# Zeroing a row table in smaller pieces, moving four scatters behind the last x, and turning step 2's rows ahead of w1's load

## The chip, the cores and the metric

The kernel runs on one core of a Trainium2 chip. The metric is the device time of one execution in microseconds (us). A kernel is compared by the median of several runs; one further execution is profiled, and the trace is of that one. The engines are PE (matrix products and transpositions), DVE (vector), ACT (activations and copies), POOL (GpSimd; it also issues the indirect DMAs) and SP (it issues the plain DMAs and the DMA transpositions, in order, waiting where it must).

## What is computed

Linear attention with exponential random features (batch 8, 8 heads, 576 tokens, head size 64, 128 features), and on its output a mixture of 8 experts where each of the 4608 tokens goes to one expert.

```python
phi = lambda x: exp(h - max(h)) / sqrt(m)        # h = x @ omega.T - |x|^2/2
kv  = einsum('bhsm,bhsd->bhmd', phi(k), v);  z = phi(k).sum(axis=2)
out = (phi(q) @ kv) / (phi(q) @ z + 1e-6)        # -> x: (4608, 512)
logits = x @ w_gate;  e = argmax(logits, axis=1);  g = softmax(logits)[e]
y[mask_e] = g[mask_e] * (relu(x[mask_e] @ w1[e]) @ w2[e])      # for each expert e
```

## The kernel before

**Attention.** `Attention.run` goes through 8 batches of 4 head pairs. Each engine's instructions run in the order in which the code is written. Of a batch, 512 tokens of each head are worked on per head (`unit_*`), the last 64 tokens of all heads together (loads `kr`, `qr` in `load_rest`, L127). k, q and v come in 256 KB loads (`load_part`, L131; `load_v`, L149) that SP issues a batch ahead into two sets of buffers. PE turns k and q (`turns`, L158), ACT copies them out (L200) and takes the exponentials (L241), POOL sums the key features (L257), DVE makes x (`pair_x`, L324 to 326), POOL copies x into rows `xr` and `xc` (L333, L336).

**Routing.** For each batch DVE and PE work out each token's expert and its place in that expert's part of a table in DRAM, `rows_by_expert` (8 parts of 4992 rows, 2056 bytes each). POOL scatters the rows of a batch into it, 128 rows to an indirect DMA (`place`, L664); `rt.move()` issues the next such scatter, so four or five belong to a batch. Not every row of a part gets a token, and the tables' rows that are read directly are zeroed before: `Experts.clear(1)`, in the batch with number 1, lets POOL zero a buffer `xg[1]` (L835) and one third of `xg[0]` (L836), and SP write `xg[1]` eight times into the table (L838).

**Experts.** `Experts.run` works in steps of up to 256 rows. Step 0 has the first 256 rows of the largest expert, step 1 the next 256 (`second`, L842, a plain DMA that waits for the scatters). From step 2 on POOL gathers a step's rows by a list of indices (`gather`, L958, two tiles of 128 rows; `gather3` a third tile) into `xg[t % 2]`. SP turns each tile by a DMA transposition (`flips`, L868) into `xt`; ACT joins the halves (`xtrans`, L976) and rounds them (`xh`, L58), DVE takes the rest (`xl`, L52). `marks(t)` copies a step's gate values (POOL, L986) and token numbers (DVE, L987) and needs all its tiles. PE makes layer 1 (L1005) and layer 2 (L1046 to 1048), with DVE splitting `w2` (L52) and making `hl` (L1020) during step 1. `next` loads the next expert's weights, 2 MB each (`dma1`, L928: w1; `dma2`, L931: w2). Results leave by scatters (L1080).

In step t, `step` issues the turning of step t + 1; `begin(t + 1)` reads it after layer 1 of step t.

Of the kernel before, what the change touches and what calls it, by code (L numbers as in the profile page):

```python
# [9 lines left out]
F32 = mybir.dt.float32  # L10
# [10 lines left out]
P = 128  # L21
B, H, S, D, M = 8, 8, 576, 64, 128
DM = H * D
E, F = 8, 1024
NT = B * S
SM = 512
SR = S - SM
NJ = SM // P
NP = H // 2
# [8 lines left out]
RW = 2 * DM + 4  # L38
# [25 lines left out]
class Attention:  # L64
# [340 lines left out]
    def pair(self, i, p, pre):  # L405

        rt, (u, w) = self.routing, self.units[i:i + 2]
        self.unit_p(*u)
        self.unit_m(*u)
        self.warm(5 * (p == 2))  # L410
        self.turns(i + 3, i - 2, pre)
        self.copies(i + 3, i - 2, pre)
        for k in range(2):
            pre.ahead(i + k - len(self.units))
        products = bool(rt.queue) and rt.queue[0] in rt.pe
        rt.some(int(products))
        rt.some(1, False)
        self.pair_kv(p - 1)
        self.pair_kvt(p - 1, self.nc.vector.tensor_copy)
        rt.some(2 + (p > B * NP - 3) - products, False)  # L420
        self.unit_e(*u, 0)
        self.pair_fold(p - 2)
        self.unit_e(*u, 1)
        self.unit_ks(*u)
        rt.move()
        self.unit_p(*w)
        self.unit_m(*w)
        self.turns(i + 4, i - 1, pre)
        self.copies(i + 4, i - 1, pre)
        self.unit_e(*w, 0)  # L430
        self.unit_e(*w, 1)
        rt.exps()
        self.unit_ks(*w)
        rt.move()
        if p % NP < NP - 1 or p == B * NP - 1: self.numbers(p - 2)

    def run(self, pre):
        self.units = [(b, h) for b in range(B) for h in [-1] + list(range(H))]
        n, rt = len(self.units), self.routing
        self.start()  # L440
        for b in range(B):
            i = b * (2 * NP + 1)
            if b:
                self.rest(i, b, pre)
                pre.clear(b)
            if b + 1 < B:
                self.load_rest(b + 1)
                self.load_main(b + 1)
            for k in range(0 if b else 2, NP):
                self.pair(i + 1 + 2 * k, b * NP + k, pre)  # L450
                if k == (0 if b else 2) and b + 1 < B:
                    self.load_v(b + 1)
        p = B * NP - 1
        self.cq.close()
        bank = lambda name: self.pt.tile([P, 2, 2, NJ * D], F32, name=name, tag="tt")
        tt = bank("tt_end")
        self.pair_kv(p)
        self.pair_kvt(p)
        self.ci.close()
        pre.banks()  # L460
        assert not rt.queue
        self.turn_q(n - 2, tt[:, :, 1])
        self.qt(n - 2, tt[:, :, 1])
        self.pair_fold(p - 1)
        self.pair_fold(p, "kv")
        rt.move(2)
        self.pair_nu(p - 1, 0)
        self.pair_x(p - 1, 0)
        self.turn_q(n - 1, tt[:, :, 0])
        self.qt(n - 1, tt[:, :, 0], self.nc.scalar.copy)  # L470
        self.pair_nu(p - 1, 1)
        self.pair_x(p - 1, 1)
        last = bank("nu_end")
        pre.fill(2)
        for a in range(2):
            self.pair_nu(p, a, last[:, a].rearrange("p k c -> p (k c)"))
        for a in range(2):
            self.pair_x(p, a)
        assert len(rt.moves) == 0
        self.ct.close()  # L480
        pre.banks2()


class Routing:
# [69 lines left out]
    def bank(self, name):  # L554
        return self.ps.tile([P, 512], F32, name=name, tag=self.tag)
# [252 lines left out]
class Experts:  # L808
# [22 lines left out]
        self.idx = [cp.tile([P, 3], U32, name=f"idx{i}") for i in range(3)]  # L831

    def clear(self, k):
        if k == 1:
            self.nc.gpsimd.memset(self.xg[1].rearrange("p a c -> p (a c)").bitcast(F32), 0.0)  # L835
            self.nc.gpsimd.memset(self.xg[0][:, 2].bitcast(F32), 0.0)  # L836
            for x in self.table.rearrange("(e n) c -> e n c", e=E):
                self.nc.sync.dma_start(x[self.T2:self.T2 + self.T3].rearrange("(a p) c -> p a c", p=P), self.xg[1])  # L838

    def second(self):  # L840
        rows = self.table.rearrange("(e n) c -> e n c", e=E)[bass.ds(self.first, 1), self.T2:2 * self.T2]
# [100 lines left out]
    def split(self, n, cs=range(8)):  # L942
        for c in cs:
            split_r(self.nc, *self.part(n, c), self.nc.scalar, self.nc.vector)
# [163 lines left out]
    def step(self, t, following, split=lambda: None):  # L1108
        engines = (ET.PE, ET.DVE, ET.Activation, ET.Pool)
        if t + 1 < NPR:  # L1110
            self.flips(t + 1)
            self.flips3(t + 1)
        split()
        kind = self.kind(t, engines)
        self.l1(t, kind)
        if t + 2 < NPR:
            self.gather(t + 2)
            self.gather3(t + 2)
        if t == 1:
            self.next(0, 2)  # L1120
        following()
        self.nc.gpsimd.drain()
        with self.tc.If(kind > 1) as pair:
            self.l2(t, 0)
            self.when(self.reg(4, t, 1, engines), lambda: self.l2(t, 1))
        with pair.Else():
            with self.tc.If(kind > 0) as short:
                self.l2half(t)
            with short.Else():
                self.l2(t, 2)  # L1130
            for a in range(2):
                self.l2(t, a)
# [11 lines left out]
    def run(self, ctx):  # L1144
        nc, rt = self.nc, self.rt
# [26 lines left out]
        self.l20(0)  # L1172
        self.xtrans(1)
        self.low(range(4, 8), nc.vector)
        self.next(0, 1)
        self.gather(2)
        self.gather3(1)
        self.marks(1)
        self.l20(1)
        self.flips3(1)  # L1180
        self.third(1)
# [49 lines left out]
```

## Time and profile before

| | |
|---|---|
| runs of the kernel before | 691.11, 692.62, 693.4 us; median 692.62 |
| the profiled execution | 690.93 us, of which the span of the trace is 689.2 us |
| mean granted clock of PE | 0.982 of full speed |
| busy share of the span | PE 94%, ACT 57%, DVE 48%, POOL 44% |
| attention | 0 to about 257 us |
| last routing, scatters, step 0 | about 257 to 285.6 us |
| steps from 1 on | 285.6 us to the end |

Times in the rows are us from the start of the span. In attention PE and ACT are both busy nearly all the time; in the steps PE alone is.

### The profile page before, as it was taken

What the parts mean: (1) busy time and instruction counts of PE and PEld (TensorE: products, weight loads), DVE (VectorE), ACT (ScalarE), POOL (GpSimd) and SP (SyncE); (2) the same over time, 40 slices, a digit from 0 to 9 for tenths busy, and PEclk for the clock granted to TensorE, in tenths of its full rate; (3) what the DMA queues carried; (4) which work ended last, traced back from release to release, by engine and by line L of the source; (5) the groups of instructions that cost most, each with busy time, mean ns of one, the idle gap of its engine ahead of it and who ended that gap; (6) DMA issues with size and microseconds to landing.
All of it is one profiled execution on the core that took longest, in us unless ns stands there. A gap on an engine that the chain in (4) does not pass through costs nothing. (4 is left out here: it accounts for less than half of the span.)

```text
span 689.2 us, 19218 instructions
## 1 busy us (share of the span) xinstructions
PE 646.5 (94%) x7123; PEld 584.5 (85%) x7123; DVE 330.7 (48%) x782; ACT 395.6 (57%) x971; POOL 300.6 (44%) x495
## 2 busy tenths in 40 slices
PE   8994999999999979986999989999999999999996
PEld 7993989898898967676889888899899899889894
DVE  3472777878877858632222235421236237222220
ACT  6993999999999953522342345431454446342421
POOL 6572698888888884321222121323201321332121
PEclk9997999999999999998999999999999999999998
DMA  8749957557474263697554025855207926843001
GB/s 219 200 170 307 258 148 235 166 161 206 134 218 157 116 196 113 172 181 188 124 101 95 31 65 169 214 118 116 62 23 192 240 64 179 245 113 51 31 18 39
DMA packets 111101, 100.55 MB, mean 146 GB/s; under 512 B 67358, under 2 KB 91934, under 8 KB 110944
## 3 DMA queue, kind: packets, MB, share of 16 engines
q1 hardware_dynamic: 100656, 68.66, 39.5%
q0 software_dynamic: 9744, 29.71, 13.8%
q8 instruction: 92, 1.51, 0.9%
q14 instruction: 65, 0.53, 0.3%
q10 hardware_dynamic: 544, 0.13, 0.1%
HBM read 64.35 MB, written 26.41 MB: 132 GB/s over the span
## 5 line engine op out<-in xcount | busy, mean ns | idle before, releaser
L1005 PE MATMUL p<-xh,w1p 128*128 128x256 f32 (+2 forms) x960 | 148.3, 297 | 5.9 <-ACTq L1085 5.2
L1005 PEld LDWEIGHTS p<-xh,w1p 128*128 128x128 f32 x960 | 135.5, 189 | 8.7 <-ACTq L1085 5.6
L1019 ACT ACTIVATE hh<-p 128x512 fp32r<-128x512 f32 (+2 forms) x84 | 43.8, 522 | 132.6 <-PE p L1005 120.8
L1080 POOL DMA_INDIRECT out_dram<-ys,idx x32 | 33.7, 1055 | 181.5 <-DVE ys L1076 90.7
L1020 DVE SCALAR_TENSOR_TENSOR hl<-p,hh 128x512 fp32r<-128x512 f32 (+2 forms) x84 | 48.1, 576 | 120.0 <-ACT hh L1019 112.4
L229 DVE TENSOR_REDUCE mx<-pp 128x8 f32<-128x1024 f32 x64 | 78.2, 1221 | 29.7 <-PE pp L222 26.6
L241 ACT ACTIVATE qp<-pp,mx 128x128 f32<-128x128 f32 x256 | 85.2, 564 | 0.0
L241 ACT ACTIVATE kp<-pp,mx 128x128 f32<-128x128 f32 x256 | 83.3, 528 | 2.2 <-DVE de L324 0.9
L1005 PE MATMUL p<-xl,w1p 128*128 128x256 f32 (+2 forms) x480 | 83.3, 295 | 0.0
L200 ACT COPY tq<-tt 128x1024 f32<-128x1024 f32 x59 | 69.9, 1184 | 15.0 <-PE tt L158 14.9
L222 PE MATMUL pp<-om_t,tq 64*128 64x128 f32 x1024 | 75.0, 286 | 1.5 <-ACT tq L203 0.7
L1005 PEld LDWEIGHTS p<-xl,w1p 128*128 128x128 f32 x480 | 70.5, 189 | 0.0
L222 PEld LDWEIGHTS pp<-om_t,tq 64*128 64x128 f32 x1024 | 62.8, 188 | 5.3 <-ACT qp L241 2.0
L958 POOL DMA_INDIRECT xg<-rows_by_expert,src x49 | 52.7, 1075 | 24.6 <-issue 23.3
L257 POOL TENSOR_TENSOR k<-kp 128x256 f32<-128x256 f32 x64 | 46.6, 728 | 35.1 <-ACT kp L241 34.1
L976 ACT COPY xw<-xt 128x1024 uint16<-128x1024 uint16 x36 | 48.6, 1349 | 15.3 <-DMA xt<-xg 15.3
L52 DVE TENSOR_TENSOR xl<-xw,xh 128x512 fp32r<-128x512 f32 x36 | 24.9, 693 | 57.7 <-ACT xh L58 49.2
L1080 POOL DMA_INDIRECT out_dram<-y,idx x6 | 6.0, 1004 | 105.7 <-DVE y L1076 57.0
L1048 PE MATMUL p_t<-w2p,hl 128*128 128x512 f32 x120 | 47.0, 392 | 1.4 <-issue 1.4
L1046 PE MATMUL p_snu<-w2p,hh 128*128 128x512 f32 x120 | 47.0, 392 | 0.4 <-issue 0.4
L1048 PE MATMUL p_snu<-w2p,hl 128*128 128x512 f32 x120 | 47.0, 391 | 0.0
L1046 PE MATMUL p_t<-w2p,hh 128*128 128x512 f32 x120 | 46.8, 390 | 0.0
(372 smaller groups left out, 1274.3 us busy)
## 6 DMA issues: line engine op xcount, KB each, us to landing
w1s<-in_moe_w_dram SPq DMA_DIRECT2D x5, 2048.0 KB
w2s<-in_moe_w_dram SPq DMA_DIRECT2D x5, 2048.0 KB
v<-in_v_dram SPq DMA_DIRECT2D x32, 256.0 KB
k<-in_k_dram SPq DMA_DIRECT2D x31, 256.0 KB
q<-in_q_dram SPq DMA_DIRECT2D x31, 256.0 KB
rows_by_expert<-xg SPq DMA_DIRECT2D x8, 771.0 KB
xg<-rows_by_expert SPq DMA_DIRECT2D x2, 514.0 KB
kr<-in_k_dram SPq DMA_DIRECT2D x16, 64.0 KB
```

The costliest lines, as they stand in the source:

```text
L200: self.nc.scalar.copy(self.pack(i, j), tt)
L222: nc.tensor.matmul(pp[:, a, n, i, :], th[r, k].rearrange("p a t -> p (a t)"), self.om[r, :], start=True, stop=True)
L229: nc.vector.tensor_reduce(out=mx[:, :, n], in_=s[("pp", h)][:, :, n], axis=AX.X, op=ALU.max, negate=True)
L241: nc.scalar.activation(x[:, j, :], pp[:, j % 2, n, j // 2, :], AF.Exp, bias=mx[:, j % 2, n, j // 2:j // 2 + 1])
L257: add = lambda o, x, y: nc.gpsimd.tensor_tensor(out=o, in0=x, in1=y, op=ALU.add)
L958: self.nc.gpsimd.indirect_dma_start(out=self.xg[t % 2][:, a], out_offset=None, in_=self.table, in_offset=bass.IndirectOffsetOnAxis(ap=self ...
L976: self.nc.scalar.copy(x.bitcast(U16).rearrange("p c (t k) -> p k c t", k=2), xt.rearrange("p (k c) t -> p k c t", k=2))
L1005: self.nc.tensor.matmul(o, w[:, i, c], x[:, i, :], start=k == 0, stop=k == len(ops) - 1)
L1019: self.nc.scalar.activation(a[:, :, :n], o[:, :, :n], AF.Relu)
L1020: low = lambda d, c: self.nc.vector.scalar_tensor_tensor(out=d, in0=o[:, :, c], scalar=0.0, in1=a[:, :, c].bitcast(F32), op0=ALU.max, op1= ...
L1046: nc.tensor.matmul(p, h, self.w2h[:, c, :], start=c == 0, stop=False)
L1048: nc.tensor.matmul(p, l, self.w2h[:, c, :], start=False, stop=c == self.NF - 1)
```

## The change

There are three parts.

1. The zeroed rows of each expert's part are 288 to 511 (224 rows, one DMA of 112 partitions by 2 rows) where they were 256 to 639 (384 rows). They are written by `blank(p)` ahead of the pairs 2 to 7, that is in the batches with numbers 0 and 1: one, one, one, two, two and one DMA. Their source is one tile of `xg[1]`, which POOL zeroes at the start; the rest of the buffers is zeroed in the batches 2 and 3.
2. In the last pair `move` issues nothing; the four scatters of the seventh batch (number 6) follow after POOL's last copies of x, ahead of the last batch's.
3. `flips(2)` stands ahead of w1's load, `next(0, 1)`, and no longer in `step(1)`.

```diff
--- before.py
+++ after.py
@@ -422,7 +422,7 @@
         self.pair_fold(p - 2)
         self.unit_e(*u, 1)
         self.unit_ks(*u)
-        rt.move()
+        rt.move(int(p < B * NP - 1))
         self.unit_p(*w)
         self.unit_m(*w)
         self.turns(i + 4, i - 1, pre)
@@ -431,7 +431,7 @@
         self.unit_e(*w, 1)
         rt.exps()
         self.unit_ks(*w)
-        rt.move()
+        rt.move(int(p < B * NP - 1))
         if p % NP < NP - 1 or p == B * NP - 1: self.numbers(p - 2)
 
     def run(self, pre):
@@ -442,11 +442,12 @@
             i = b * (2 * NP + 1)
             if b:
                 self.rest(i, b, pre)
-                pre.clear(b)
+            pre.clear(b)
             if b + 1 < B:
                 self.load_rest(b + 1)
                 self.load_main(b + 1)
             for k in range(0 if b else 2, NP):
+                pre.blank(b * NP + k)
                 self.pair(i + 1 + 2 * k, b * NP + k, pre)
                 if k == (0 if b else 2) and b + 1 < B:
                     self.load_v(b + 1)
@@ -463,7 +464,6 @@
         self.qt(n - 2, tt[:, :, 1])
         self.pair_fold(p - 1)
         self.pair_fold(p, "kv")
-        rt.move(2)
         self.pair_nu(p - 1, 0)
         self.pair_x(p - 1, 0)
         self.turn_q(n - 1, tt[:, :, 0])
@@ -476,7 +476,8 @@
             self.pair_nu(p, a, last[:, a].rearrange("p k c -> p (k c)"))
         for a in range(2):
             self.pair_x(p, a)
-        assert len(rt.moves) == 0
+        rt.move(NJ)
+        assert not rt.moves
         self.ct.close()
         pre.banks2()
 
@@ -831,11 +832,21 @@
         self.idx = [cp.tile([P, 3], U32, name=f"idx{i}") for i in range(3)]
 
     def clear(self, k):
-        if k == 1:
-            self.nc.gpsimd.memset(self.xg[1].rearrange("p a c -> p (a c)").bitcast(F32), 0.0)
-            self.nc.gpsimd.memset(self.xg[0][:, 2].bitcast(F32), 0.0)
-            for x in self.table.rearrange("(e n) c -> e n c", e=E):
-                self.nc.sync.dma_start(x[self.T2:self.T2 + self.T3].rearrange("(a p) c -> p a c", p=P), self.xg[1])
+        zero = self.nc.gpsimd.memset
+        if k == 0:
+            zero(self.xg[1][:, :1].bitcast(F32), 0.0)
+        elif k == 2:
+            zero(self.xg[1][:, 1:].bitcast(F32), 0.0)
+        elif k == 3:
+            zero(self.xg[0][:, 2].bitcast(F32), 0.0)
+
+    def blank(self, p):
+
+        known = NT // 2 // E
+        n = (2 * self.T2 - known) // 2
+        for e in {2: (0,), 3: (1,), 4: (2,), 5: (3, 4), 6: (5, 6), 7: (7,)}.get(p, ()):
+            rows = self.table.rearrange("(e n) c -> e n c", e=E)[e, known:2 * self.T2]
+            self.nc.sync.dma_start(rows.rearrange("(a p) c -> p a c", p=n), self.xg[1][:n, :1].to_broadcast([n, 2, RW]))
 
     def second(self):
         rows = self.table.rearrange("(e n) c -> e n c", e=E)[bass.ds(self.first, 1), self.T2:2 * self.T2]
@@ -1108,7 +1119,8 @@
     def step(self, t, following, split=lambda: None):
         engines = (ET.PE, ET.DVE, ET.Activation, ET.Pool)
         if t + 1 < NPR:
-            self.flips(t + 1)
+            if t > 1:
+                self.flips(t + 1)
             self.flips3(t + 1)
         split()
         kind = self.kind(t, engines)
@@ -1172,10 +1184,11 @@
         self.l20(0)
         self.xtrans(1)
         self.low(range(4, 8), nc.vector)
-        self.next(0, 1)
         self.gather(2)
         self.gather3(1)
         self.marks(1)
+        self.flips(2)
+        self.next(0, 1)
         self.l20(1)
         self.flips3(1)
         self.third(1)
```

In the following lists, `rows_by_expert<-xg1` is a zeroing write, `kr_2`, `qr_2`, `k_2`, `q_2`, `v_2` are loads of the batch with number 2, `vz` the last 64 tokens of v. This is SP's queue before, from the loads of v of batch 1 on:

```order
L149 DMA vz10_160<-in_v_dram 64x4x64
L149 DMA vz11_161<-in_v_dram 64x4x64
L131 DMA v_1_653<-in_v_dram 128x2x256 x4
L838 DMA rows_by_expert<-xg1_81 128x3x1028 x8
L127 DMA kr_2_854<-in_k_dram 64x4x64 x2
L127 DMA qr_2_857<-in_q_dram 64x4x64 x2
L131 DMA k_2_861<-in_k_dram 128x2x256
```

And now, from the same place to the loads of batch 2:

```order
L849 DMA rows_by_expert<-xg1_81 112x2x1028
L149 DMA vz10_160<-in_v_dram 64x4x64
L149 DMA vz11_161<-in_v_dram 64x4x64
L131 DMA v_1_655<-in_v_dram 128x2x256 x4
L849 DMA rows_by_expert<-xg1_81 112x2x1028
L127 DMA kr_2_847<-in_k_dram 64x4x64 x2
L127 DMA qr_2_850<-in_q_dram 64x4x64 x2
L131 DMA k_2_854<-in_k_dram 128x2x256
```

Eight writes stood between v of batch 1 and `kr` of batch 2; one stands there now and one ahead of v. Of the other six, one stands ahead of v of batch 2, two behind it, and three behind the write of `xr` of batch 0 and ahead of `kr` of batch 3.

POOL at the end of attention, before; `k2_7_7` and `ks_7_3` are the key sums of the last head, `xc_6` the rows of the seventh batch, `xc_7` and `xq_7` those of the last:

```order
L664 DMA rows_by_expert<-xc_6_4845,rt_pos_85 39936x1028
L257 TENSOR_TENSOR k2_7_7_5666<-kp_7_7_5656 128x256
L257 TENSOR_TENSOR ks_7_3_5626<-k2_7_7_5666 128x128
L257 TENSOR_TENSOR ks_7_3_5626<-ks_7_3_5626,kz1_200 128x128
L664 DMA rows_by_expert<-xc_6_4845,rt_pos_85 39936x1028
L333 COPY xr_7_4355<-x_7_4354 128x2x64
L336 COPY xc_7_5540<-x_7_4354 128x4x128 x2
L664 DMA rows_by_expert<-xc_6_4845,rt_pos_85 39936x1028 x2
```

And now, with the end of the copies and the scatters behind them:

```order
L257 TENSOR_TENSOR k2_7_7_5664<-kp_7_7_5654 128x256
L257 TENSOR_TENSOR ks_7_3_5627<-k2_7_7_5664 128x128
L257 TENSOR_TENSOR ks_7_3_5627<-ks_7_3_5627,kz1_200 128x128
L333 COPY xr_7_4356<-x_7_4355 128x2x64
...
L336 COPY xc_7_5541<-x_7_4355 128x4x128 x2
L549 COPY xq_7_5836<-rt_id_116 128x1
L665 DMA rows_by_expert<-xc_6_4846,rt_pos_85 39936x1028 x4
L665 DMA rows_by_expert<-xc_7_5541,rt_pos_85 39936x1028 x4
```

The last head's sums lose the scatter ahead of them, and the four scatters of `xc_6` now stand directly ahead of those of `xc_7`.

SP ahead of step 1, before; `xg1` has the rows of step 1, `xg0` those of step 2, `xt0` and `xt1` are step 2's turned rows:

```order
L868 DMA_TRANSPOSE xt2_5948<-xg1_81 128x8x128
L868 DMA_TRANSPOSE xt3_5949<-xg1_81 128x8x128
...
L928 DMA w1s_75<-in_moe_w1_dram 128x4x1024
...
L868 DMA_TRANSPOSE xt0_5946<-xg0_80 128x8x128
L1033 UNCONDITIONAL_BRANCH x2
L868 DMA_TRANSPOSE xt1_5947<-xg0_80 128x8x128
...
L931 DMA w2s_76<-in_moe_w2_dram 128x8x512
```

And now:

```order
L879 DMA_TRANSPOSE xt2_5949<-xg1_81 128x8x128
L879 DMA_TRANSPOSE xt3_5950<-xg1_81 128x8x128
L879 DMA_TRANSPOSE xt0_5947<-xg0_80 128x8x128
L879 DMA_TRANSPOSE xt1_5948<-xg0_80 128x8x128
...
L939 DMA w1s_75<-in_moe_w1_dram 128x4x1024
```

The two transpositions of step 2 follow those of step 1 at once, and w1's load stands behind all four.

## Rows read from the trace of the kernel before

**Rows 1.** Timeline, 50 to 72: start, duration, engine, instruction, [idle before <-releaser].
```profile
53.17 0.39 PE L276 MATMUL kv<-kp_-1_832,vz 128*64 128x128 f32 x4
...
64.99 0.77 PE L158 MATMUL tt<-ident,kr 64*128 64x64 f32 x4 [9.47 <-DMA kr<-in_k_dram]
...
67.01 1.01 ACT L200 COPY tq<-tt 128x1024 f32<-128x1024 f32 x1 [10.94 <-PE tt L158]
...
71.44 1.01 ACT L200 COPY tq<-tt 128x1024 f32<-128x1024 f32 x1 [1.22 <-PE tt L158]
```
**Rows 2.** Timeline of SP's queue, 0 to 110; the duration is the issuing.
```profile
42.56 9.44 SPq L838 DMA_DIRECT2D rows_by_expert<-xg  x8
52.10 3.44 SPq L127 DMA_DIRECT2D kr<-in_k_dram  x2
```
**Rows 3.** Timeline of POOL, 20 to 110.
```profile
23.63 0.45 POOL L257 TENSOR_TENSOR ks<-ks,kz 128x128 f32<-128x128 f32 x1
...
41.15 1.39 POOL L835 MEMSET xg<- 128x1542 f32 x1
...
82.87 0.73 POOL L257 TENSOR_TENSOR k<-kp 128x256 f32<-128x256 f32 x1 [1.37 <-ACT kp L241]
```
**Rows 4.** Windows: length, busy PE, PEld, DVE, ACT, POOL (count), clock, DMA, GB/s.
```profile
60.00:70.00 10.00, 5.01 (x58) 4.31 (x60) 1.36 (x6) 2.99 (x10) 0.78 (x2) 0.50 1.09 272
```
**Rows 5.** Timeline of all engines, 283 to 331.
```profile
281.71 1.34 ACT L976 COPY xw<-xt 128x1024 uint16<-128x1024 uint16 x1 [2.27 <-DMA xt<-xg]
...
283.01 1.06 POOL L958 DMA_INDIRECT xg<-rows_by_expert,src  x1 [0.30 <-issue]
...
284.97 0.62 ACT L58 CAST xh<-xw 128x512 fp32r<-128x512 f32 x1
...
285.69 1.50 POOL L958 DMA_INDIRECT xg<-rows_by_expert,src  x1 [0.30 <-issue]
...
289.59 0.16 DVE L987 SCALAR_TENSOR_TENSOR idx<-src,xg 128x3 uint32<-128x3 uint32 x1 [0.88 <-DMA xg<-rows_by_expert,src]
...
291.82 1.25 POOL L958 DMA_INDIRECT xg<-rows_by_expert,src  x1 [0.31 <-issue]
...
298.10 0.68 DVE L1020 SCALAR_TENSOR_TENSOR hl<-p,hh 128x512 fp32r<-128x512 f32 x1
...
301.72 0.19 POOL L986 COPY gt<-xg 128x3 f32<-128x3 f32 x1 [3.27 <-DMA xg<-rows_by_expert,src]
...
303.44 0.50 PE L1048 MATMUL p_t<-w2p,hl 128*128 128x512 f32 x1 [1.40 <-issue]
...
306.45 1.35 ACT L976 COPY xw<-xt 128x1024 uint16<-128x1024 uint16 x1 [9.03 <-DMA xt<-xg]
...
315.21 0.58 PE L1005 MATMUL p<-xh,w1p 128*128 128x256 f32 x1 [5.17 <-ACTq L1085]
```
**Rows 6.** Timeline of SP's queue, 270 to 420.
```profile
278.38 2.74 SPq L868 DMA_TRANSPOSE xt<-xg  x2
...
290.31 9.38 SPq L868 DMA_TRANSPOSE xt<-xg  x2
```
**Rows 7.** Windows of the steps 1 and 2, columns as in rows 4.
```profile
285.64:296.63 10.99, 10.99 (x98) 10.99 (x97) 8.78 (x16) 6.50 (x12) 6.93 (x6) 1.00 0.81 263
...
315.21:328.67 13.46, 12.95 (x97) 12.66 (x98) 3.11 (x6) 2.75 (x5) 4.30 (x5) 0.84 0.70 146
328.67:339.60 10.93, 10.93 (x50) 9.01 (x49) 2.64 (x5) 4.81 (x6) 2.05 (x3) 1.00 0.76 137
```
**Rows 8.** Timeline of all engines, 249 to 287.
```profile
252.74 0.28 PE L298 MATMUL fold<-ones,ks 128*64 128x1 f32 x4 [1.28 <-POOL ks L257]
...
261.28 0.19 POOL L548 COPY xq<-rt_id 128x1 int32<-128x1 int32 x1
...
265.68 0.99 POOL L664 DMA_INDIRECT rows_by_expert<-xc,rt_pos  x1 [4.21 <-DVE f_ch L726]
...
270.87 0.98 POOL L664 DMA_INDIRECT rows_by_expert<-xq,rt_pos  x1 [0.30 <-issue]
```

## The prediction

> **What bounds the kernel now.** I began with the page's busy shares: PE 94%, so that little is to be won but where PE stands still. The slices of the page show two such places, and I opened the timeline of all engines at each.
>
> The first is in attention. ACT, which hardly rests there otherwise, stands still for 10.94 us before its copy at 67.01, and once more for 1.22 us before the one at 71.44; PE waits 9.47 us for the load of `kr`, the remainder of batch 2 [rows 1]. The timeline of SP's queue says why that load is late: SP issues the eight zeroing writes from 42.56 on and `kr` only at 52.10, and then `kr` lands at 64.99, behind the 6.3 MB of the writes [rows 1, 2]. The reader is to see that SP did nothing before 42.56: the writes wait for POOL's zeroing of the buffer at 41.15 [rows 3], and everything behind them in the queue waits too. [...]
>
> The second is at the start of step 2. PE stands still for 5.17 us before 315.21 [rows 5]. The chain goes back over ACT, which waits 9.03 us for the first turned tile at 306.45, to SP's two transpositions, which take 9.38 us to be issued from 290.31 on, behind w1's 2 MB [rows 5, 6]. Two transpositions with nothing ahead of them take 2.74 us to issue, and the first is used at 281.71, 3.33 us after its issue at 278.38 [rows 5, 6]. Of the clock: in the window that holds step 2's first layer it is 0.84 on average, and this layer takes 13.46 us where step 1's takes 10.99 [rows 7].
>
> **Part 1, the zeroing.** The eight writes become eight of 224 rows for 384, 3.7 MB for 6.3, and `kr` of batch 2 has two of them ahead of it, not eight. Nothing makes SP wait between the loads of batch 1 and those of batch 2 but POOL's first zeroing, and that stands behind the sums that end at 24.08 [rows 3]; so batch 2's loads can be issued soon after that, and PE wants `kr` at 64.99 - 9.47 = 55.52. The gain is both of ACT's waits, 10.94 + 1.22 = 12.16 us, **taken as 12.2**. The price: POOL zeroes the same 2056 numbers to a partition as before, where 1542 of them took 1.39 us, so the largest of the three zeroings, 1028, should take under that; it falls ahead of batch 2's sums, where POOL waits 1.37 us for ACT anyway [rows 3]. Without that cover it would delay sums that PE needs two pairs later, so I price it at nothing; its bound is 1.4. Each write also stands ahead of a load. The worst place is the three together ahead of batch 3's `kr`: the 6.3 MB held `kr` up for 64.99 - 42.56 = 22.4 us, so 1.38 MB cost 4.9, but that load has a batch's length of lead. Taken as 0, bound 4.9.
>
> **Part 2, the scatters.** One of POOL's scatters stands ahead of the last head's key sums, and PE waits 1.28 us for these [rows 8]. Without it everything that follows on PE and DVE, to the last x, comes 1.28 us earlier, as POOL's last copy does: it ends at 261.47 - 1.28 = 260.19. But now four scatters follow it before the last batch's. One takes (270.87 - 265.68) / 4 = 1.30 us, so the last five begin at 260.19 + 0.30 + 4 x 1.30 = 265.69, where they began at 265.68 [rows 8]. They end when they ended, and so do the plain load and the transpositions of step 1 that wait for them. Step 1's first layer begins when ACT has the second half rounded, at 284.97 + 0.62 = 285.59; PE starts at 285.64 [rows 5, 7]. So PE arrives 1.28 us early and waits 1.28 us. **Taken as 0.** The bounds: 1.3 lost if x does not come earlier, 1.3 won if the scatters go closer together. The 4.21 us for which POOL waited before 265.68 is the cover; without it the cost would be 5.2.
>
> **Part 3, the transpositions.** A gather comes in 289.59 - 285.69 = 3.90 us after its issue, as the wait for the third one shows; by that the first tile of step 2, issued at 283.01, is there at 286.91 [rows 5]. SP has nothing else to do from 281.12 on [rows 6], so the first transposition is issued then, the second some 1.3 us later; alone they would land at 290.2 and 291.6. ACT wants them after layer 1, at 297.42 (its 9.03 us of waiting began there). So the wait goes, with about 6 us to spare. All that PE lost is the stretch from 285.64 to 328.67, 43.03 us, less two first layers and a second at full speed, 2 x 10.99 + 10.93 = 32.91: **10.1 us** [rows 7]. Two things come off.
>
> The transpositions now run while the third gather of that group is coming in, for which DVE waits before all its work in step 1. A gather beside transpositions took longer: the next one, issued at 291.82 with w1's load and transpositions around it, was waited for until 301.72, 9.9 us [rows 5]. So this delay lies between 0 and 6.0 us. I take 2.5, nearer the low end, since the third gather is issued 1.2 us ahead of the first transposition, and undisturbed it is in, at 289.59, before that one could land. DVE's last `hl` ends at 298.78 and PE wants it for the last quarter of the second layer's first half, at 296.63 + 0.75 x 5.47 = 300.73 [rows 5, 7]; so 1.95 us of delay are free, and 2.5 cost 0.55. The ends: 0 and 4.05.
>
> PE also stands still for 1.40 us at 303.44 with nothing that the profile names [rows 5]. This is inside the 10.1. It falls into the busiest stretch of the transfers, which is thinned out, but nothing shows that it goes; I keep half, 0.7. So part 3 brings 10.1 - 0.55 - 0.7 = **8.9**.
>
> w1's load goes out behind the transpositions, a few us late; it is for the next expert, and no row of these stretches waits for it. SP comes to w2's load no later, as it is no longer held for 9.38 us. What is late next are step 3's turned rows, which stand behind w2's load in both kernels and are wanted 9 us sooner. ACT did not wait for them; at worst PE's 5.17 us come again there.
>
> [...]
>
> **The sum.** 12.2 + 0 + 8.9 = 21.1 us. The profiled execution took 690.93 (its span of 689.2 and 1.73 around it) and would take 669.8; it lies 1.7 below the median of 692.62, from which the same sum gives **671.5**.
>
> **Rivals.**
> [...] Chance 0.13.
> *A zeroing write still stands ahead of a load that is wanted* (for it: 3.7 MB more in the batches 0 and 1, some in one go; against it: the lead). Price 4.9: 676.4. Chance 0.07.
> *The wait for turned rows does not go, but moves to step 3*, which would be the change not doing what it is made for in its third part. Price 5.17 and 2.5 for the clock: 679. Chance 0.07.
> *Slower than before*: SP now waits at the first zeroing write for POOL, with v of batch 1 behind it. If that zeroing came late, `kv` of batch 1, which PE makes at 53.17 [rows 1], would wait, a us for a us. If a load takes 5 us (an estimate, a little over the 3.90 of a gather), it begins to cost when the zeroing ends after 48, and decides the sign when it ends 21 us later, at 69. POOL is free at 24.08 [rows 3], and only a wait that the trace does not show could put it off so far. Time 693 or more. Chance 0.02.
>
> **How the numbers follow.** The sum as worked out has 0.68, and its own range, from part 2's bounds and the small ones of part 3, is 668.5 to 674. A time below 668, with all of the 10.1 and a part of the 1.28 won, has 0.03. Leaving out that, the slower case and most of the 679 gives the range 668 to 678. What a measurement can tell from no change is 0.3%, 2.1 us, as the runs before differ by 2.3. All cases but the slower one and a residue of unknown ones lie well below that: faster 0.97, same 0.01, slower 0.02.
>
> **What would show it.** Part 1: ACT without a wait over 2 us from 25 to 240, the clock at 1.00 from 55 to 70, and the last x some 13 us earlier. Part 2: no wait of PE for POOL before the last fold, nine scatters in a row 1.30 us apart, and PE waiting about 1.3 us before step 1. Part 3: transpositions of step 2 issued within 3 us of each other and ahead of w1's load, ACT at once on them after step 1's layer 1, no wait of PE at step 2 and full clock. It is wrong if PE waits for a load in the batches 1 to 3, if DVE's `idx` of step 1 comes over 4 us after the third gather's usual arrival, or if step 3's rows are waited for.

## The result and the profile after

The changed kernel took 671.32 us (median of 6 runs, 669.71 to 674.16), the kernel before 691.06 beside it: ratio 0.972, 95% interval 0.968 to 0.975. Later runs gave 0.969 (0.965 to 0.973); one execution among them that took 1269.1 us is left out of that ratio. The predicted 671.5 stands. The profiled execution took 670.34 us with a span of 668.6; its clock is 0.996.

**Attention.** SP's queue after, from its timeline, where the duration is the issuing; it answers to [rows 2]:

```profile
24.42 0.36 SPq L849 DMA_DIRECT2D rows_by_expert<-xg  x1
...
30.16 0.47 SPq L849 DMA_DIRECT2D rows_by_expert<-xg  x1
30.72 2.59 SPq L127 DMA_DIRECT2D kr<-in_k_dram  x2
...
39.74 0.47 SPq L849 DMA_DIRECT2D rows_by_expert<-xg  x1
...
46.28 2.32 SPq L849 DMA_DIRECT2D rows_by_expert<-xg  x2
...
55.31 2.19 SPq L849 DMA_DIRECT2D rows_by_expert<-xg  x3
57.54 2.73 SPq L127 DMA_DIRECT2D kr<-in_k_dram  x2
```

`kr` of batch 2 is issued at 30.72, where it was issued at 52.10. Between 50 and 72 us no wait of PE or ACT is over 0.5 us. The windows after (columns as in [rows 4]) show full speed there, and then the steps 1 and 2 by layers:

```profile
271.81:283.17 11.36, 11.29 (x97) 11.09 (x97) 4.18 (x9) 6.34 (x12) 6.28 (x7) 1.00 0.68 140
283.17:297.08 13.91, 12.38 (x51) 8.77 (x49) 9.06 (x16) 4.79 (x6) 5.62 (x5) 1.00 1.02 360
297.08:309.49 12.41, 11.47 (x98) 11.01 (x96) 2.56 (x4) 2.27 (x4) 3.26 (x4) 1.00 0.69 136
309.49:320.44 10.95, 10.95 (x50) 9.01 (x49) 2.63 (x5) 4.81 (x6) 3.07 (x4) 1.00 0.92 152
55.00:70.00 15.00, 14.25 (x315) 13.52 (x313) 13.03 (x29) 14.68 (x48) 11.08 (x22) 1.00 0.89 260
```

**The last routing.** Rows of PE and POOL from the timeline; they answer to [rows 8]:

```profile
236.31 0.66 PE L276 MATMUL kv<-kp,v 128*64 128x128 f32 x8 [1.47 <-issue]
...
238.74 0.42 PE L298 MATMUL fold<-ones,ks 128*64 128x1 f32 x8
...
246.25 0.19 POOL L549 COPY xq<-rt_id 128x1 int32<-128x1 int32 x1
246.58 1.00 POOL L665 DMA_INDIRECT rows_by_expert<-xc,rt_pos  x1
...
256.80 1.02 POOL L665 DMA_INDIRECT rows_by_expert<-xq,rt_pos  x1 [0.30 <-issue]
```

PE's wait for POOL is gone, and nine scatters follow each other at 1.28 us. The row of PE's last `kv` before, which serves below as a mark, is:

```profile
248.80 0.66 PE L276 MATMUL kv<-kp,v 128*64 128x128 f32 x8 [1.47 <-issue]
```

**Steps 1 and 2.** From the timelines of all engines and of SP; they answer to [rows 5, 6]:

```profile
264.43 16.36 SPq L879 DMA_TRANSPOSE xt<-xg  x4
...
272.10 1.17 POOL L1091 DMA_INDIRECT out_dram<-ys,idx  x1 [14.28 <-DVE ys L1087]
...
276.77 1.00 POOL L969 DMA_INDIRECT xg<-rows_by_expert,src  x1 [0.30 <-issue]
...
280.65 0.17 DVE L998 SCALAR_TENSOR_TENSOR idx<-src,xg 128x3 uint32<-128x3 uint32 x1 [5.23 <-DMA xg<-rows_by_expert,src]
...
282.79 0.00 SPq L939 DMA_DIRECT2D w1s<-in_moe_w_dram  x1
...
284.05 1.33 ACT L987 COPY xw<-xt 128x1024 uint16<-128x1024 uint16 x1
...
285.14 0.50 PE L1059 MATMUL p_t<-w2p,hl 128*128 128x512 f32 x1 [0.70 <-DVE hl L1031]
...
303.91 1.20 PE L1016 MATMUL p<-xh,w1p 128*128 128x256 f32 x8 [0.93 <-ACT hh L1030]
```

The four transpositions stand ahead of w1, and ACT takes step 2's rows at 284.05 without a wait. But `idx` comes 8.84 us after step 1's start at 271.81, for 3.95 before; PE then waits 0.70 us for `hl`. The gather itself took 3.88 us, for 3.90 before. It was issued late, behind a scatter that waited for DVE's `ys`.

### The profile page after: what moved, and what is told of

The parts are those of the page before. It is cut to its first block, busy times and chain, and to the rows that moved or that the text cites. A ratio compares the mean times of both kernels' runs of the same rounds, so it can differ in the third digit from the quotient of the medians.

```text
span 668.6 us, 19215 instructions
## 1 busy us (share of the span) xinstructions
PE 641.5 (96%) x7123; PEld 579.8 (87%) x7123; DVE 331.3 (50%) x782; ACT 394.1 (59%) x971; POOL 300.1 (45%) x496
## 3 DMA queue, kind: packets, MB, share of 16 engines
q0 software_dynamic: 9744, 29.71, 13.7%
q8 instruction: 92, 1.51, 1.0%
## 5 line engine op out<-in xcount | busy, mean ns | idle before, releaser
L257 POOL TENSOR_TENSOR k<-kp 128x256 f32<-128x256 f32 x64 | 46.5, 727 | 23.2 <-ACT kp L241 21.1
L1058 PE MATMUL p_t<-w2p,hh 128*128 128x512 f32 x120 | 46.9, 391 | 0.4 <-issue 0.4
L1057 PE MATMUL p_t<-w2p,hh 128*128 128x512 f32 x120 | 46.8, 390 | 0.0
```

What stands on the lines that cost most here:

```text
L257: add = lambda o, x, y: nc.gpsimd.tensor_tensor(out=o, in0=x, in1=y, op=ALU.add)
L1057: nc.tensor.matmul(p, h, self.w2h[:, c, :], start=c == 0, stop=False)
L1058: nc.tensor.matmul(p, h, self.w2l[:, c, :], start=False, stop=False)
```

## The experiments

The ratios come from several runs of each kernel, the traces from one execution each, and the two must be held apart here. So this table gives the ratio and, for the one trace of each kernel, four stretches in us, cut at the first row of each: from ACT's first exponential to step 1's first product on PE (A), from there to step 2's (1), to step 3's (2), and to the end (rest).

```
kernel                      ratio to before (95%)    A      1     2     rest
before                      1                        276.6  29.6  24.4  349.6
changed                     0.972 (0.968 to 0.975)   262.9  25.3  23.4  348.1
changed, again              0.969 (0.965 to 0.973)   263.8  22.4  21.9  349.2
part 1 alone                0.980 (0.976 to 0.984)   262.3  27.4  25.9  349.6
part 2 alone                0.997 (0.994 to 0.999)   276.5  28.0  25.0  348.5
part 3 alone                0.988 (0.984 to 0.993)   274.7  22.6  28.8  347.9
parts 1 and 3               0.973 (0.969 to 0.976)   261.4  22.0  26.3  349.5
parts 1 and 3, again        0.974 (0.972 to 0.977)   263.0  22.5  21.9  347.5
fewer rows, one burst       0.991 (0.988 to 0.994)   267.1  30.0  25.4  349.6
384 rows, spread            0.985 (0.981 to 0.989)   262.9  29.6  25.0  347.7
step 3's turning held       0.975 (0.971 to 0.979)   262.8  22.5  22.3  351.4
turning ahead, every step   0.972 (0.970 to 0.975)   263.8  25.6  23.8  348.7
turning four times          0.982 (0.979 to 0.984)   262.5  26.7  24.0  349.0
gathers ahead               0.978 (0.976 to 0.981)   261.5  23.8  24.7  347.7
```

What the parts do lies in A, 1 and 2; the rest differs by up to 4 us from trace to trace, in no order that follows the parts. Undisturbed, 1 and 2 take some 21.9 each.

**Part 1 alone.** The first part of the diff, nothing else:

```diff
+            pre.clear(b)
...
+                pre.blank(b * NP + k)
```

> The kernel before with part 1 alone (fewer rows zeroed, spread over two batches). Both theories: both of ACT's waits go, 10.94 + 1.22 = 12.2 us, so a ratio near 0.982, and everything behind attention as before, PE's 5.17 us before step 2 among it. What it tells: under 11 would mean that one of the writes costs something, over 13 that the zeroing cost more than the two waits that the trace names.

Ratio 0.980: 689.7 x 0.0199 = 13.7 us (11.1 to 16.3). Stretch A is 14.3 shorter. The two waits made 12.2 of it; the rest lies outside them, but 12.2 is inside the interval too.

**Part 2 alone.**

```diff
-        rt.move()
+        rt.move(int(p < B * NP - 1))
...
-        rt.move(2)
...
+        rt.move(NJ)
```

> The kernel before with part 2 alone (all nine scatters of the last batch behind the last x). Theory of the prediction: 0, since the last five scatters begin when they did. Rival, from the trace of the changed kernel, where POOL's last copy came 15.0 us earlier and not 12.2 + 1.3: x comes some 2.5 us earlier than before, so the last scatters, the plain load and step 1 come about 1.3 us earlier: 1.3 us faster, ratio 0.998. A third reading: with nine scatters in a row DVE's chain of the plan is stretched by 4 to 5 us, as in the changed kernel from 251 to 260 us, whatever the other parts do; then DVE's idx of step 1 comes later against step 1's start than the 3.95 us of before, and this trace shows it.

Ratio 0.997: 2.2 us (0.6 to 3.8), the rival's 1.3 rather than 0. Stretch A of its trace is only 0.2 shorter, but PE came late to its last `kv` there, at 252.52 for 248.80, of which 1.2 us lie in a part of A that the edit does not touch and the rest ahead of A. Counted from that `kv`, POOL's last copy came 2.5 us earlier than before, the last five scatters (the first at 267.95) 1.5, and step 1 began 1.3 earlier:

```profile
252.52 0.66 PE L276 MATMUL kv<-kp,v 128*64 128x128 f32 x8 [1.37 <-issue]
...
262.47 0.19 POOL L548 COPY xq<-rt_id 128x1 int32<-128x1 int32 x1
...
288.03 1.21 PE L1005 MATMUL p<-xh,w1p 128*128 128x256 f32 x8 [0.90 <-ACT xh L58]
```

That is the rival's mechanism, in its sizes. DVE's plan was not stretched: 14.5 us.

**Part 3 alone.**

```diff
-            self.flips(t + 1)
+            if t > 1:
+                self.flips(t + 1)
...
-        self.next(0, 1)
...
         self.marks(1)
+        self.flips(2)
+        self.next(0, 1)
```

> The kernel before with part 3 alone (step 2's transpositions ahead of w1's load). Theory of the prediction: 8.9 us faster, ratio 0.987, with idx of step 1 coming 2.5 us later than before because the third gather runs beside the transpositions. Rival: the late idx of the changed kernel (8.84 us after step 1's start, 3.95 before) does not come from the transpositions, as the gather itself took 3.88 us, but from its late issue, which is part 2's doing. Then idx stands here as before, and the part brings 9.4 to 10.1.

Ratio 0.988: 8.1 us (5.0 to 11.2). `idx` came 4.46 us after step 1's start; the third gather took 288.51 - 284.45 = 4.06, so the transpositions did not hold it. Both readings lie in the interval. Yet in its trace the two steps from 284.1 took 51.4 us, 2.6 less than before and not 9 less. The timeline of PE and a window of its trace say where it went:

```profile
306.64 0.28 PE L1005 MATMUL p<-xh,w1p 128*128 128x256 f32 x1
310.74 1.87 PE L1005 MATMUL p<-xh,w1p 128*128 128x256 f32 x7 [3.82 <-issue]
...
306.64:324.49 17.85, 14.03 (x97) 13.75 (x96) 2.56 (x4) 2.27 (x4) 5.30 (x6) 0.81 0.65 124
```

One product of step 2, then 3.82 us of nothing that the profile names, then a lower granted clock, 0.81 on average over the layer: 17.85 us for a layer of 10.9. In the same trace a 16384-byte packet of an instruction queue took 3.17 us, from 306.21 to 309.38; PE went on 1.36 us later. In the kernel before such a packet took 4.08 us and ended at 302.08, 1.36 us ahead of the unnamed 1.40 at 303.44 [rows 5]. In the middle such packets take 1.06 us in the fourteen traces; one in ten takes over 1.35, and 39 of the 1288 take 1.5 to 2.7.

**Parts 1 and 3**, the changed kernel without part 2:

```diff
-        rt.move(int(p < B * NP - 1))
+        rt.move()
...
+        rt.move(2)
...
-        rt.move(NJ)
-        assert not rt.moves
+        assert len(rt.moves) == 0
```

> The kernel before with parts 1 and 3, the changed kernel without part 2. Theory of the prediction: part 2 is worth nothing, so this is as fast as the changed kernel, about 19.7 us faster than before, with DVE's idx late as there. Rival: nine scatters in a row hold up DVE's plan and ACT's relus of the first step; without them the plan ends as it did before against its start, idx comes some 4 us earlier against step 1's start, and part 3 brings its 9 us and more: 12.2 + 9.4 = 21.6 us faster, ratio 0.969, that is some 2 us under the changed kernel.

Ratio 0.973. `idx` came 4.11 us after step 1's start and the plan took 14.7 us, as the rival said; but the time was not under the changed kernel's, and in its trace PE had the unnamed wait here too:

```profile
292.07 0.28 PE L1016 MATMUL p<-xh,w1p 128*128 128x256 f32 x1
...
295.04 1.87 PE L1016 MATMUL p<-xh,w1p 128*128 128x256 f32 x7 [2.68 <-issue]
...
292.07:307.42 15.35, 12.67 (x97) 12.39 (x96) 2.56 (x4) 2.27 (x4) 5.29 (x6) 0.89 0.65 150
```

**The changed kernel again**, without an edit, for a second trace.

> The changed kernel once more, for a second trace of it beside the runs of this call. In its first trace DVE's plan took from 249.37 to 268.74 us, 19.4 us, where the kernel before, part 2 alone and parts 1 and 3 took 14.5 to 14.7. Theory: this is a property of the program, so the plan takes over 18 us again, idx of step 1 comes over 7 us after step 1's start, and PE has no unnamed wait before step 2. Rival: it was one execution's bad luck; then the plan takes under 16 us, idx comes some 4 us after step 1's start, and what PE then loses at step 2's start is an unnamed wait of 2 to 4 us, as in parts 1 and 3.

Ratio 0.969. The rival, for this trace: the plan took 14.5 us, `idx` came 3.26 us after step 1's start, and no unnamed wait came in its place. The windows of the second trace are what part 3 looks like when nothing goes wrong:

```profile
284.50:295.48 10.98, 10.98 (x51) 9.01 (x49) 3.30 (x7) 4.82 (x6) 2.08 (x3) 1.00 1.13 343
295.48:306.40 10.92, 10.92 (x98) 10.92 (x97) 2.56 (x4) 2.28 (x4) 3.72 (x5) 1.00 0.45 121
```

**Step 3's transpositions held back**, on parts 1 and 3 (a scrap transfer that reads `hh` stands ahead of them):

```diff
-            if t > 1:
+            if t > 2:
                 self.flips(t + 1)
-            self.flips3(t + 1)
+            if t != 2:
+                self.flips3(t + 1)
...
         self.l1(t, kind)
+        if t == 2:
+            self.nc.sync.dma_start(self.scrap, self.hh[:1, :8].bitcast(F32))
+            self.flips(3)
+            self.flips3(3)
```

> Parts 1 and 3, with step 3's transpositions held back until ACT has made the first hh of step 2: a 32-byte transfer that reads hh stands ahead of them in SP's queue. Theory: PE's unnamed wait at the start of step 2 (2.68 us at 295.04 in parts 1 and 3, 3.82 us at 310.74 with part 3 alone, 1.40 us at 303.44 in the kernel before) is code that arrives late because transpositions are running: in the kernel before and with part 3 alone a 16384-byte packet of an instruction queue took 4.08 and 3.17 us and ended 1.36 us before PE went on, beside 1.0 to 1.1 us for such packets elsewhere. With the transpositions held back the wait goes and with it the low clock behind it: some 4 us less than parts 1 and 3, ratio to the kernel before about 0.967. Rival: PE waits there for something else, such as a register or a branch; then the wait stays at 2 to 3 us and the ratio at 0.972 to 0.973. If step 3's rows then come late, PE waits before step 3 instead.

The unnamed wait is not in this trace, and the steps 1 and 2 took 44.8 us for 48.3. But the ratio is 0.975 (0.971 to 0.979): nothing was won in the runs. In its trace the rest took 351.4 us, with a wait of PE of 1.94 us for ACT's `xw` in a later step. Inconclusive on the cause, since the second trace of parts 1 and 3, below, has no such wait either.

**Fewer rows in one burst**, on the kernel before:

```diff
-                self.nc.sync.dma_start(x[self.T2:self.T2 + self.T3].rearrange("(a p) c -> p a c", p=P), self.xg[1])
+                self.nc.sync.dma_start(x[288:512].rearrange("(a p) c -> p a c", p=112), self.xg[1][:112, :2])
```

> The kernel before with one edit: the eight zeroing writes cover 224 rows for 384 (3.7 MB for 6.3), at their old place, all eight in one burst behind POOL's zeroing at 41.15. Theory of bytes: kr lands at 42.56 + 22.4 x 3.67 / 6.29 = 55.6 us, as early as PE wants it (55.52), so nearly all of part 1's gain comes from the bytes: ratio 0.982 to 0.984. Rival: the zeroing at 41.15 and the queue behind it hold kr as well; then kr lands near 58 to 60 and the gain is half, ratio 0.986 to 0.990.

Ratio 0.991 (0.988 to 0.994): 6.4 us, about half of part 1. The time is the rival's or a little over it, but `kr` came earlier than the 58 to 60 that the rival gave and later than the 55.6 of the theory of bytes. `kr` was issued at 51.95, no earlier than before, since SP takes 9.35 us to issue the eight writes, for 9.44 with the larger ones; PE used it at 56.98. Rows of PE and ACT from its timeline and one of its windows:

```profile
56.98 0.57 PE L158 MATMUL tt<-ident,kr 64*128 64x64 f32 x4 [2.65 <-DMA kr<-in_k_dram]
...
59.23 1.01 ACT L200 COPY tq<-tt 128x1024 f32<-128x1024 f32 x1 [3.48 <-PE tt L158]
...
64.14 1.01 ACT L200 COPY tq<-tt 128x1024 f32<-128x1024 f32 x1 [1.70 <-PE tt L158]
...
60.00:65.00 5.00, 5.00 (x77) 4.78 (x76) 2.91 (x8) 3.30 (x11) 3.09 (x7) 0.65 1.05 317
```

After PE's wait of 2.65 us the granted clock was 0.65 on average from 60 to 65, and ACT's two waits make 5.18 of the former 12.16.

**384 rows, spread**, the kernel before with part 1's places and its old size:

```diff
-        ... [e, known:2 * self.T2]
+        ... [e, known:known + self.T3]
```

> The kernel before with part 1's spreading alone: POOL's early zeroing and the writes ahead of the pairs 2 to 7, but each of 384 rows as before (6.3 MB). Theory: kr of batch 2 has two writes ahead of it, not eight, 1.57 MB or 5.6 us, and a batch's length of lead, so that the whole gain of part 1 is there without fewer bytes: ratio as part 1 alone, 0.980. Rival: the bytes matter too, kr of batch 2 or 3 or a v comes late by some us: ratio 0.983 or more, with a wait of PE or ACT for a load over 2 us between 25 and 110 us.

Ratio 0.985, 10.4 us (7.9 to 12.9). The ratio is the rival's, but its sign is missing: no wait for a load over 2 us stands in the trace, and its stretch A is that of part 1 alone within 0.6. So the spreading alone does most or all of part 1; the two intervals overlap, so what the bytes add is not settled.

**Transpositions ahead of w1's load in every step**, on the changed kernel:

```diff
         self.third(t)
+        if t + 1 < NPR:
+            self.flips(t + 1)
         self.change(t, 1)
...
-            if t > 1:
-                self.flips(t + 1)
```

> The changed kernel with part 3 made general: in every step the transpositions of the next step's rows are issued in begin, ahead of the load of w1 that a new expert needs, and no longer behind it. In the second trace of the changed kernel w1 is issued at 397.78, 497.54 and 550.35 and two transpositions right behind it take 7.6 us to issue (398.53, 551.11) where two without it take 3.14 (522.97). Theory: PE's waits for ACT's xw (1.7 to 1.9 us in nearly all traces, in steps with a new expert) go, and part of the low clock behind them (0.95 on average over 36 us around such a step, 1.8 us): 2 to 3.5 us under the changed kernel, ratio 0.965 to 0.968. Rival: those waits come from ACT's own work in such steps, the splitting of w1, and nothing changes: ratio 0.970 as the changed kernel over both calls.

Ratio 0.972 (0.970 to 0.975), the time of the rival. The two transpositions now took 3.50 us to issue, ahead of w1's load, and PE's wait for `xw` was there all the same:

```profile
383.73 3.50 SPq L879 DMA_TRANSPOSE xt<-xg  x2
...
393.07 0.47 PE L1072 MATMUL p_skv<-w2p,hh 128*128 128x512 f32 x1 [1.86 <-ACT xw L987]
...
402.37 0.41 SPq L939 DMA_DIRECT2D w1s<-in_moe_w_dram  x1
```

The order in time speaks against both readings: this wait ends some 9 us before w1's load goes out. The changed kernel's first trace has the same order (391.40 and 400.88), and there ACT begins to split w1 only at 394.57. What ACT did just before was its last `hh` (389.69) and then, without a wait, the copying of `xw` (390.02).

**Four times the transpositions in three steps:**

```diff
-            if t > 1:
-                self.flips(t + 1)
+            for _ in range(4 if t in (2, 8, 9) else int(t > 1)):
+                self.flips(t + 1)
```

> The changed kernel with the transpositions of the next step's two tiles issued four times over in the steps 2, 8 and 9 (the same data to the same place). Theory: transpositions delay the code that PE runs, so PE has unnamed waits of 1 to 4 us in these steps and packets of the instruction queue there take over 2 us for 1.0: 2 to 8 us slower than the changed kernel. Rival: they need other transfers beside them, gathers or a weight load, to do that, as at the start of step 2 in the kernel before; then there are no unnamed waits over 0.8 us in the steps 8 and 9, and the time is within 2 us of the changed kernel unless a step's rows come late.

Ratio 0.982 (0.979 to 0.984), some 8 us over the changed kernel, the upper end of what the theory forecast. But its trace has no unnamed wait of PE over 0.8 us in the steps 2, 8 and 9, though one instruction packet took 2.12 us there: transpositions alone did not make the wait in this execution. The trace (673.7 us) is the fastest of its four runs (the others 676.8 to 680.0), so it does not show where those lost, and the theory is neither shown nor refuted by it.

**Parts 1 and 3 again**, without an edit:

> Parts 1 and 3 once more, for a second trace and more runs beside the changed kernel. Theory: the unnamed wait of PE at the start of step 2 (2.68 us) belongs to the way in which the transfers fall there, so it is there again, at 1 us or more, and from step 1's start to step 3's start takes 47 to 49 us for 43.8 undisturbed. Rival: it comes by chance, as the slow plan of the changed kernel's first trace did; then step 3 starts 44 to 45 us after step 1. On part 2, which this leaves out: theory of the prediction, ratio within 0.002 of the changed kernel's (0.970 over both calls); rival, 0.973 to 0.974.

The rival, in this trace: 44.4 us from step 1 to step 3, no unnamed wait. It is the fastest of its runs (665.7; the others 671.0 to 676.0). The ratio, 0.974, with 0.973 in the first runs, for 0.972 and 0.969 of the changed kernel: part 2 comes to some 2 us beside the others, but each of the four ratios has an interval of about 2.5 us on either side, so that these runs alone do not tell it from nothing.

**The gathers ahead of step 0's scatter**, on the changed kernel:

```diff
+        nc.gpsimd.tensor_copy(self.y3[:1, :1], self.xt[3][:1, 0, :2].bitcast(F32))
+        self.gather(2)
+        self.gather3(1)
         self.l20(0)
...
-        self.gather(2)
-        self.gather3(1)
```

> The changed kernel with the three gathers of step 1's third tile and step 2's rows ahead of step 0's first result scatter in POOL's queue; one number is copied from the second turned tile of step 1 ahead of them, so that they start when that tile is there and not beside its transposition. In the changed kernel they stood behind that scatter, which waited for DVE's ys at 271.34 and so for DVE's plan. Three of four traces of kernels with all three parts have a plan of 19.4 to 20.8 us and idx 8.8 to 10.5 us after step 1's start. Theory: the gathers go out near 269 for 273.57, idx comes near 275.5, PE has no wait for hl in step 1, and where the plan is slow 3 to 4 us are won: ratio 0.965 to 0.967. Rival: step 2's transpositions and the loads now come earlier against PE, as without part 2, and PE gets an unnamed wait at the start of step 2 for them: ratio 0.970 to 0.974, as the changed kernel.

Ratio 0.978 (0.976 to 0.981): 5 us worse than the changed kernel, worse than both readings. The plan was not slow in this trace, and the third gather now was. Rows of POOL from its timeline:

```profile
269.64 1.07 POOL L969 DMA_INDIRECT xg<-rows_by_expert,src  x1 [1.00 <-DVE xl L52]
...
272.69 1.49 POOL L969 DMA_INDIRECT xg<-rows_by_expert,src  x1 [0.30 <-issue]
...
278.89 0.19 POOL L997 COPY gt<-xg 128x3 f32<-128x3 f32 x1 [3.37 <-DMA xg<-rows_by_expert,src]
```

6.2 us from issue to use, 3.5 to 4.2 in the other traces; w1's load then went out at 277.24 and PE waited 1.86 us at the start of step 2. The trace is the fastest of its five runs (668.7; the others 670.7 to 674.8), so it does not show all that they lost.

## Why the prediction was right

The total was right: 21.1 predicted, 19.5 to 21.3 by the two ratios. The waits that the parts were made for went as described. The terms were not equally right.

**Part 1, 12.2.** Right. The waits went as described, and the granted clock is 1.00 from 55 to 70, where it was 0.50 from 60 to 70 [rows 4]; ACT's second wait, 1.22, came at the end of that stretch and is gone with it. PE came to its last `kv` at 236.31 for 248.80, 12.5 us earlier, and the part alone measures 13.7 (11.1 to 16.3). It was priced by ACT's two waits alone, which leaves out some 1.5 to 2 us. PE's waits for DVE's x at `kv` fell from 3.7 to 1.9 us in total in its trace, which is of that size; that they are the rest is not shown. The price of nothing for the writes holds: no wait for a load over 2 us stands in the traces, not even with 6.3 MB.

**Part 2, 0.** Within its bounds of -1.3 to 1.3 by the traces, and low by the runs (2.2 alone, from 0.6 to 3.8). The step at fault is that x comes 1.28 us earlier: it counts PE's one wait and not the other scatters, at 252.96, 255.52 and 256.81 before, that stood ahead of or between POOL's last copies; that these are the rest is argued from their place. In the changed kernel POOL's last copy came 261.28 - 246.25 = 15.0 us earlier, 2.5 more than the 12.5 that attention had won by then. So the last five scatters begin not when they began but sooner: 251.71 for 265.68 is 14.0 earlier, 1.5 beyond the 12.5, and step 1's start, 271.81 for 285.64, 1.3 beyond. Part 2 alone shows the same three numbers, 2.5, 1.5 and 1.3.

**Part 3, 8.9.** The mechanism was right: transpositions ahead of w1, no wait of ACT, and where nothing else happens 44.3 to 44.4 us for 54.0, so 9.6 to 9.7 of the 10.1. Two terms were mis-sized. The third gather, 2.5 us late by the prediction, is late by 0.3 us at most in eight of the nine traces with part 3 (3.88 to 4.16 us against 3.90); only where it was issued earlier did it take 6.2. That transpositions behind a gather hold it up is not seen in those eight. And PE's unnamed 1.40 us, of which half was kept, does not shrink: it is 0 in some executions and, at the start of step 2, 2.68 to 3.82, with 1.8 to 3.1 us of low clock behind it, in others (15.35 and 17.85 us for a layer of 10.9). So the part brings 2.6 to 9.7 us by the execution, 8.1 alone by the ratio and, beside part 1, 0.980 - 0.9735 = 0.0065, or 4.5 us, where each of the two ratios has some 2.6 us on either side.

So the closeness of the sum owes something to luck: by these values terms too small (part 1, with 13.7, and part 2, with 2) stood beside one too large (part 3, with 4.5). That 13.7 + 2 + 4.5 = 20.2 comes near the total is no check, as each value is taken with the parts before it in place. Measured alone, the parts come to 13.7 + 2.2 + 8.1 = 24.0, more than the whole brought; the difference is within the noise of the three.

**What the unnamed wait is** is argued, not shown. That PE waits for code that comes late is the author's guess, from a DMA queue that the pages name instruction (q8, 92 packets and 1.51 MB in each kernel's trace). For it: all three packets of this queue of over 3 us in these traces end shortly ahead of an unnamed wait's end: 1.36 us with the kernel before and with part 3 alone, and with 384 rows spread one of 3.01 us ends at 288.1 where a wait of 0.78 us ends at 289.58. When a packet ends says more than how long it took. PE has an unnamed wait of 1.37 to 1.48 us at its last `kv` in every one of the fourteen traces, whatever the packets do. Besides these there are eleven unnamed waits of over 0.7 us, and ten of them end 1.28 to 1.50 us after a 16384-byte packet ended, though only 5% of PE's instructions start at such a distance (1.20 to 1.55 us). With part 2 alone (1.72 us at 306.55) the packet took only 1.07 us, and ended 1.28 us ahead. The eleventh speaks against it: with parts 1 and 3 the packet before the wait took 1.04 us and ended 2.5 us ahead. If it is the code, what makes it late is open. Six of the ten stand in attention, at 52 to 53 and 102 to 103 us, where SP issues no transposition. In the steps the fourfold kernel's one trace did not have the wait, though its runs were as slow as transpositions that delay the code would have made them.

**Steps that were wrong though the time was not.** `idx` over 4 us after its usual time was named as a sign that the prediction is wrong; it came, and not for the reason given. In the first trace of the changed kernel DVE's plan, the chain that makes the lists of rows to gather, took 19.4 us for 14.5, and the third gather was issued late behind a scatter that waited for what DVE did after it.

## What to carry to other kernels

The burst of writes cost its place in the issuing queue as well as its bytes: eight writes held SP for 9.4 us with 384 rows each and with 224 alike, and spreading them over two batches won more than making them smaller (10.4 us and 6.4). The term priced by waits that the trace names came out; the one that kept an unnamed wait in it should have been carried as a range. And a stretch that varies by 4 us from one execution to the next has to be judged by several runs: of two traces of the same program here, one showed 48.6 us and the other 44.3.

## What the runs showed of the hardware

**In some executions a chain of waits crawls.** In three of the five traces with all three parts (the changed kernel's first, transpositions ahead in every step, four times the transpositions), DVE's plan took 19.4 to 20.8 us, in the other two, and in all nine traces without one of the parts, 14.5 to 14.7. The work is the same; but six to eight times in the plan DVE waits 0.3 to 1.3 us for its own last result, where in the other traces no such wait of the plan is over 0.15, and ACT's relu stands still. First the rows of DVE and ACT in the first trace of the changed kernel:

```profile
252.26 0.17 DVE L733 TENSOR_TENSOR f_c<-f_c,f_odd 128x8 f32<-128x8 f32 x1 [0.43 <-DVE f_six L732]
252.99 0.20 DVE L734 TENSOR_TENSOR f_c<-f_c,f_six 128x8 f32<-128x8 f32 x1 [0.56 <-DVE f_c L733]
253.69 0.22 DVE L735 TENSOR_TENSOR f_m<-rt_low,f_c 128x64 f32<-128x64 f32 x1 [0.51 <-DVE f_c L734]
...
259.56 1.08 ACT L914 ACTIVATE h<-p 128x512 f32<-128x512 f32 x2 [8.10 <-remote]
```

and the same in its second trace:

```profile
252.89 0.17 DVE L733 TENSOR_TENSOR f_c<-f_c,f_odd 128x8 f32<-128x8 f32 x1
253.09 0.17 DVE L734 TENSOR_TENSOR f_c<-f_c,f_six 128x8 f32<-128x8 f32 x1
253.29 0.22 DVE L735 TENSOR_TENSOR f_m<-rt_low,f_c 128x64 f32<-128x64 f32 x1
...
255.43 0.60 ACT L914 ACTIVATE h<-p 128x512 f32<-128x512 f32 x1 [2.86 <-PE p L910]
```

It begins while POOL issues nine scatters in a row (246.58 to 257.82) and ends at 259.5, soon after the last. It is not seen where five or four follow each other, but part 2 alone, the changed kernel's second trace and the one with the gathers ahead have nine too and no such plan. What sets it off stays open; nine scatters with a pause between them were not tried.

**Another pace at full clock.** Step 1's layer 1 goes at 1.41 us for each twelve products in six of the fourteen traces (part 3 alone: 285.76 to 287.18 to 288.59) and at 1.36 in the others (parts 1 and 3: 271.60 to 272.96 to 274.32), with a granted clock of 1.00 in both. It goes by the execution and not by the program: the changed kernel's first trace has 1.36 and its second 1.41. No run here says why.
